# Second head's maxima written into operand rows by a multiply, and a per-partition scalar for the second layer's scale

## The chip, the cores and the metric

The kernel runs on one core of one Trainium2 chip (trn2). The metric is the device time of the whole program in microseconds. Engines are called by their profile names: PE is TensorE (PEld its weight loads), DVE is VectorE, ACT is ScalarE, POOL is GpSimd, SP is SyncE, which here only issues DMAs. L959 is line 959 of the kernel before.

## The reference

Masked attention over 2 batches and 8 heads (768 tokens, 64 columns a head), in which a query sees the keys of its own cluster alone, then two dense layers on the 1536 tokens.

```python
def _attn_ref(q, k, v, centroids):                     # q, k, v: (2, 8, 768, 64)
    q_assign = argmax(einsum(q_n, c_n)); k_assign = argmax(einsum(k_n, c_n))   # 16 clusters
    mask = q_assign[:, :, :, None] == k_assign[:, :, None, :]
    scores = np.where(mask, scale * q @ k.T, -1e9)
    scores = scores - np.max(scores, axis=-1, keepdims=True)
    attn = np.exp(scores)
    attn = attn / (np.sum(attn, axis=-1, keepdims=True) + 1e-09)
    return attn @ v

def _moe_ref(x, w_in, w_out):                          # x: (1536, 512), inner width 2048
    h = x @ w_in
    g = h * (1.0 / (1.0 + np.exp(-1.702 * h)))
    return g @ w_out

def _moe2_ref(x, w_in, w_out, g_ln):                   # inner width 1024
    h = x @ w_in
    e = np.exp(h - np.max(h, axis=-1, keepdims=True))
    solu = h * (e / (np.sum(e, axis=-1, keepdims=True) + 1e-09))
    mu, var = mean and variance of solu along its row
    return (((solu - mu) / np.sqrt(var + 1e-06) * g_ln) @ w_out)
```

## The kernel before

The attention works on 16 heads `u` (pairs `p = u // 2`). Keys and queries of a head lie in two operand tiles, with the tokens along the free dimension: `OP1` holds the high parts of K and Q in partitions 0 to 63, the cluster rows in 64 to 79 and rows for the maxima from partition `KR` = 96 on; `OP2` holds the mixed high and low parts. A pair's operand tiles are used again two pairs later. A head is cut into `NU` = 9 units `m` of 512 columns. For each head the kernel first finds the maximum of each query's masked scores: nine products `peak` (L903, tile `sm`) and nine reductions `peak_max` (L914), then `peak_all` (L922) joins them to a 128x6 tile `nm` and `peak_turn` (L926) turns it on PE to 6x128.

From there the heads differ. Head 0 multiplies the turned tile with the identity, so that row `KR + j` of its Q operand holds the maxima of block `j` and zeros elsewhere (`peak_rows`, L931, on DVE). It does this in two steps, the first four blocks after six of nine units, the rest after all nine. Its scores then contract over rows 0 to `KE` = 102. Every other head copies the turned tile to `mr` (`peak_copy`, L943), and SP moves it by a DMA of 3 KB into one row, `KR` (`peak_row`, L947, recorded at L644 by the helper `move`); its scores contract over 97 rows. The rows of K that face them hold ones, in all six rows of all four operand tiles (L502). The subtraction of the maximum thus happens inside the score products (`score`, L958 and L959, tile `st`). ACT takes the exponential (L967) and casts it to a half precision high part (L972), POOL or DVE subtracts to get the low part (L976), and `value` (L991 to L995) multiplies both with V.

The order of all this is made by a planner at build time. Each operation is a task with a cost per engine, a due time and predecessors (`add`); `Plan.order` takes at each step the earliest possible task, by due time among those that are ready together, keeps account of the PSUM banks (`take`), and emits each engine's queue in that order. The engines then run their queues strictly in order. A changed task can change the order of everything behind it until the attention and the first layer's first three groups of tokens end. The maxima of head `u` are due about one head ahead of its scores (`n0 = (u - 1) * NU - LEAD`).

Behind the planner's part stand loops whose order is written out. `project` (L1308) is the first layer's second product, `solu` (L1372) the second layer's activation, on one tile `t` of 128 tokens (`NT` = 12 tiles). The last loop (L1487) emits per tile: `products(t)`, 48 matmuls on PE; `flip(t - 2)`, the DMA transposes of the finished tile, from SP (for the last tile PE transposes, L1425); `store(t - 3)`, 48 matmuls, the scaling on ACT (L1449) and the DMA out; then `solu(t)`. In `solu`, DVE reduces the maximum (L1376, L1378), multiplies it by the scale `r` of the token group (L1379), ACT takes the exponential with it as bias (L1383), DVE makes 1/sum (L1385, L1388), multiplies by `r` (L1389) and forms the product and its sum (L1392, L1396), ACT sums the squares (L1402), DVE and POOL make the root (L1404 to L1407), DVE normalises (L1408), ACT casts (L1410), and POOL subtracts to get the low part (L1412; DVE for the last tile). Each of these waits for the one before it. `r` comes from `factor` (L1351), which multiplies two [128, 1] columns of a scalar tile once per group (L1356).

Of the kernel before, what the change touches and what calls it, by code (L numbers as in the profile page):

```python
# [15 lines left out]
ALU = mybir.AluOpType  # L16
# [5 lines left out]
def kernel(  # L22
# [21 lines left out]
    nc = tc.nc  # L44
    P = 128
# [12 lines left out]
    KR = 96  # L58
# [22 lines left out]
    TXM = 1  # L81
# [2 lines left out]
    VDA = -20  # L84
    VDB = 1
    LDUE = -8
    URGENT = 0.35
    DEPTH = 1.5
    COLD, WARM = 8.0, 36.0
# [405 lines left out]
    def operands(u):  # L495
        s, i = u // 2 % NS, u % 2
        return OP1[s][i][:, 1, :], OP1[s][i][:, 0, :], OP2[s][i][:, 0, :], OP2[s][i][:, 1, :]
# [418 lines left out]
    def peak_all(u, e=None):  # L916

        n = slice(0, 4 if e == 0 else NJ)
        nms[u] = st_p.tile([P, NJ], F32, tag="nm", name="nm")
        if e == 0:  # L920
            nc.vector.memset(nms[u][:, 4:], 0.0)
        nc.vector.tensor_reduce(out=nms[u][:, n], in_=nma[u][:, n], op=ALU.min, axis=AX.X)  # L922
# [2 lines left out]
        t["tile"] = bank(t)  # L925
        nc.tensor.transpose(t["tile"][0:NJ, 0:P], nms.pop(u), ident)  # L926

    def peak_rows(t, e):

        a, b = (0, 4) if e == 0 else (4, NJ)  # L930
        nc.vector.tensor_tensor(  # L931
            out=operands(0)[0][KR:KE, a * P:b * P].rearrange("p (j n) -> p j n", n=P),
            in0=t["tile"][0:NJ, 0:P].rearrange("p (o n) -> p o n", o=1).to_broadcast([NJ, b - a, P]),
            in1=ident[0:NJ, a:b].rearrange("p (j o) -> p j o", o=1).to_broadcast([NJ, b - a, P]),
            op=ALU.mult,
        )
# [14 lines left out]
    def score(t, u, m):  # L951

        Q1, K1, Q2, K2 = operands(u)
        t["tile"] = bank(t)
        n = KE if u == 0 else KR + 1
        for kt, cs, at in cut(m):
            ks = slice(kt * P, (kt + 1) * P)
            nc.tensor.matmul(t["tile"][:, at], K2[:, ks], Q2[:, cs], start=True, stop=False)  # L958
            nc.tensor.matmul(t["tile"][:, at], K1[0:n, ks], Q1[0:n, cs], start=False, stop=True)  # L959
# [75 lines left out]
    def peaks_of(u):  # L1035
        p, i = divmod(u, 2)
        n0 = (u - 1) * NU - LEAD if u else -40
        ready = [T["PH", p, i]] + [T["PC", p, i, s] for s in range(2)]
        for m in range(NU):
            a = T["SM", u, m] = add(  # L1040
                dict(PE=0.21), n0 + m, lambda t, m=m: peak(t, u, m), after=ready + ([T["PC", 0, 0, 2]] if u == 0 and (m > 5 or m % 3 == 2) else []),
                take="sm",
            )
            T["SX", u, m] = add(
                dict(DVE=0.63), n0 + m + 1, lambda t, m=m, a=a: peak_max(a, u, m),
                after=[a, at("NM", u - 2), T["SX", u, m - 1] if m else None], frees=a,
            )
        for e in range(2 if u == 0 else 0):
            n = 6 if e == 0 else NU
            a = T["NM", u] = add(  # L1050
                dict(DVE=0.13), n0 + n, lambda t, e=e: peak_all(u, e), after=[T["SX", u, m] for m in range(n)] + [at("RW", u)],
            )
            a = T["TR", u] = add(dict(PE=0.06), n0 + n - 4, lambda t: peak_turn(t, u), after=[a], take="tx")
            T["RW", u] = T["RW", u, e] = add(
                dict(DVE=0.35 + 0.25 * (1 - e)), n0 + n - 4, lambda t, a=a, e=e: peak_rows(a, e), after=[a], frees=a
            )
        if u:
            a = T["NM", u] = add(
                dict(DVE=0.07), n0 + NU, lambda t: peak_all(u),
                after=[T["SX", u, m] for m in range(NU)] + [at("TR", u - 2)],  # L1060
            )
            a = T["TR", u] = add(dict(PE=0.06), n0 + NU + -1, lambda t: peak_turn(t, u), after=[a], take="ex")
            a = add(
                dict(ACT=0.25, DVE=0.2), n0 + NU + 1, lambda t, a=a: peak_copy(dict(a, eng=t["eng"]), u),
                after=[a, at("RW", u - 1)], frees=a,
            )
            T["RW", u] = add(dict(SP=(0.65, 0.05)), n0 + NU - 18, lambda t: peak_row(u), after=[a, at("ST", u - 4, NU - 1)])
# [3 lines left out]
    def scores_of(u):  # L1071
        p, i = divmod(u, 2)
        for m in range(NU):
            n = u * NU + m
            d = n if u else n - SOON
            a = T["ST", u, m] = add(
                dict(PE=0.47), d, lambda t, m=m: score(t, u, m),
                after=[T["RW", u, int(m % 3 == 2)] if u == 0 else T["RW", u]] + [T["PB", p, i, e] for e in range(2)], take="st" if u or m >= TXM else "tx",
            )
            o = a  # L1080
            a = T["EX", n] = add(
                dict(ACT=0.5), d, lambda t, m=m, a=a: exponential(a, u, m),
                after=[a] + ([] if stays(n) else held[-NP32:][:1] if len(held) >= NP32 else []), frees=None if stays(n) else a,
            )
            a = add(
                dict(ACT=0.52) if stays(n) else dict(ACT=0.52, DVE=0.36), n + 2, lambda t, m=m: cast(t, u, m),
                after=[a, at("AV", n - NPH)], tail=not stays(n), shared=True,
            )
            T["RE", n] = add(
                dict(DVE=0.62) if stays(n) else dict(POOL=1.11), n + 1, lambda t, m=m: rest(t, u, m), after=[a],  # L1090
                frees=o if stays(n) else None, tail=not stays(n),
            )
            if not stays(n):
                held.append(T["RE", n])
            todo.append((u, m))
            if m in ENDS:
                g = list(todo)
                todo.clear()
                head = [x for x, y in g if y == 0]
                a = add(  # L1100
                    dict(PE=AVC * len(g)), n + ADUE, lambda t, g=g: [value(t, *x) for x in g],
                    after=[T["RE", x * NU + y] for x, y in g] + [T["VL", x // 2] for x, _ in g] + [at("AV", g[0][0] * NU + g[0][1] - 1)],
                    take="av" if head else None, tail=True, kind="av",
                )
                for x, y in g:
                    T["AV", x * NU + y] = a
# [244 lines left out]
    def factor(t):  # L1351

        n = t * P // TB
        if n not in rho2:
            rho2[n] = scalar()
            nc.vector.tensor_tensor(out=rho2[n], in0=rho[n], in1=w2.i, op=ALU.mult)  # L1356
        return rho2[n]

    def products(t):
# [12 lines left out]
    def solu(t, hs):  # L1372
# [3 lines left out]
            nc.vector.tensor_reduce(out=m2[:, i], in_=h, op=ALU.max, axis=AX.X, negate=True)  # L1376
        nm = s_p.tile([P, 1], F32, tag="nm2", name="nm2")
        nc.vector.tensor_reduce(out=nm, in_=m2, op=ALU.min, axis=AX.X)  # L1378
        nc.vector.tensor_tensor(out=nm, in0=nm, in1=r, op=ALU.mult)  # L1379
        e = slots[:, t % NL, :]  # L1380
        sm = s_p.tile([P, 2], F32, tag="sm2", name="sm2")
        for h, s, i in hs:
# [3 lines left out]
            out=ri, in0=sm[:, 0:1], scalar1=sm[:, 1:2], scalar2=1e-9, op0=ALU.add, op1=ALU.add  # L1386
        )
        nc.vector.reciprocal(ri, ri)  # L1388
        nc.vector.tensor_tensor(out=ri, in0=ri, in1=r, op=ALU.mult)  # L1389
        tot = s_p.tile([P, 2], F32, tag="tot", name="tot")  # L1390
        for h, s, i in hs:
            nc.vector.scalar_tensor_tensor(  # L1392
# [142 lines left out]
```

## Time and profile before

| | |
|---|---|
| median of 3 runs | 630.42 us |
| lowest, highest | 629.82, 632.25 us |
| the profiled execution's own time | 631.68 us |
| its span, first to last instruction | 629.9 us |
| busy: PE, DVE, ACT, POOL | 604.0, 456.9, 391.8, 250.0 us |
| mean granted clock of TensorE | 0.992 |

The busy times are sums over stages of different kinds: attention to about 235 us, the first layer to about 510 us (its last stretch mixed with the second layer's first tiles), the second layer to the end. PE's busy time is 96% of the span, but a PE in an idle stretch or at a lower granted clock costs time, and such stretches are few and lie in two places, near the end and between 40 and 52 us. A row of a timeline gives start, duration, engine, line, operation and tiles, and in brackets the idle time before it and what ended that.

### The profile page before, as it was taken

What the parts mean: (1) busy time and instruction counts of PE and PEld (TensorE: products, weight loads), DVE (VectorE), ACT (ScalarE), POOL (GpSimd) and SP (SyncE); (2) the same over time, 40 slices, a digit from 0 to 9 for tenths busy, and PEclk for the clock granted to TensorE, in tenths of its full rate; (3) what the DMA queues carried; (4) which work ended last, traced back from release to release, by engine and by line L of the source; (5) the groups of instructions that cost most, each with busy time, mean ns of one, the idle gap of its engine ahead of it and who ended that gap; (6) DMA issues with size and microseconds to landing.
All of it is one profiled execution on the core that took longest, in us unless ns stands there. A gap on an engine that the chain in (4) does not pass through costs nothing. (4 is left out here: it accounts for less than half of the span.)

```text
span 629.9 us, 12832 instructions
## 1 busy us (share of the span) xinstructions
PE 604.0 (96%) x4879; PEld 395.5 (63%) x4879; DVE 456.9 (73%) x1003; ACT 391.8 (62%) x782; POOL 250.0 (40%) x215
## 2 busy tenths in 40 slices
PE   7989999999999989999999999999999999999977
PEld 6767787888888765556654666666665544444424
DVE  6878989999898858999988033566866356566662
ACT  3589998999999986678777035435335334443432
POOL 8139998758678971224221015200000212222220
PEclk9998999999999999999999999999999999999989
DMA  5897977879797116444520000260500312524241
GB/s 139 203 234 154 211 150 172 191 168 192 163 189 166 44 39 169 143 139 163 170 99 1 1 2 2 67 199 3 167 1 1 34 34 54 98 50 101 51 101 50
DMA packets 78786, 67.93 MB, mean 108 GB/s; under 512 B 61642, under 2 KB 64548, under 8 KB 78724
## 3 DMA queue, kind: packets, MB, share of 16 engines
q1 hardware_dynamic: 78724, 67.11, 44.9%
q8 instruction: 38, 0.62, 0.4%
q14 instruction: 24, 0.20, 0.1%
HBM read 34.64 MB, written 3.15 MB: 60 GB/s over the span
## 5 line engine op out<-in xcount | busy, mean ns | idle before, releaser
L976 POOL TENSOR_TENSOR ph<-p,ph 128x512 f16<-128x512 f32 x115 | 139.4, 1233 | 49.2 <-ACT ph L972 28.4
L1316 PE MATMUL yps<-g,reg 128*128 128x384 f16 x768 | 127.6, 326 | 1.0 <-DVE reg L232 0.9
L1156 PE MATMUL hps<-xT,reg 128*128 128x384 f16 x768 | 126.2, 326 | 1.5 <-DVE g L1167 1.5
L1316 PEld LDWEIGHTS <-reg 128*128 128x128 f16 x768 | 74.7, 98 | 52.4 <-DVE reg L232 4.4
L1156 PEld LDWEIGHTS <-reg 128*128 128x128 f16 x768 | 75.0, 98 | 50.5 <-issue 1.7
L914 DVE TENSOR_REDUCE nma<-sm 128x1 f32<-128x512 f32 x144 | 96.3, 680 | 8.4 <-PE sm L903 7.8
L1177 POOL TENSOR_TENSOR g<-g,g 128x384 f16<-128x384 f32 x40 | 41.7, 1044 | 123.8 <-ACT g L1172 123.8
L967 ACT ACTIVATE p<-st 128x512 f32<-128x512 f32 x114 | 68.6, 609 | 6.4 <-PE st L959 5.2
L958 PE MATMUL st<-OP 128*128 128x256 f32 (+1 forms) x191 | 69.3, 374 | 2.5 <-ACT p L967 1.3
L1406 POOL TENSOR_TENSOR rs<-va,mhalf 128x1 f32<-128x1 f32 x12 | 6.6, 551 | 158.9 <-DVE va L1404 158.9
L972 ACT CAST ph<-p 128x512 f16<-128x512 f32 x109 | 67.4, 630 | 0.4
L1365 PE MATMUL h<-reg,xT 128*128 128x512 f16 x288 | 64.1, 379 | 0.0
L959 PE MATMUL st<-OP 97*128 97x512 f32 (+3 forms) x191 | 63.0, 342 | 0.0
L995 PE MATMUL av<-vh,ph 128*128 128x65 f16 x576 | 61.1, 195 | 1.6 <-POOL ph L976 1.6
L991 PE MATMUL av<-vh,ph 128*128 128x65 f16 x576 | 61.9, 194 | 0.0
L994 PE MATMUL av<-vh,ph 128*128 128x64 f16 x576 | 61.2, 193 | 0.0
L991 PEld LDWEIGHTS <-ph 128*128 128x128 f16 x576 | 52.8, 99 | 11.2 <-issue 9.5
L903 PE MATMUL sm<-OP 80*128 80x512 f32 x192 | 57.6, 361 | 1.6 <-DVE nma L914 0.8
L1441 PEld LDWEIGHTS <-g 128*128 128x128 f16 x312 | 30.7, 99 | 39.0 <-DMA g<-g 6.6
L995 PEld LDWEIGHTS <-ph 128*128 128x128 f16 x576 | 53.6, 97 | 2.0 <-POOL ph L976 2.0
L994 PEld LDWEIGHTS <-ph 128*128 128x128 f16 x576 | 53.7, 97 | 0.2
L208 ACT ACTIVATE junk<-reg 128x512 bf16<-128x512 f32 x48 | 30.4, 633 | 30.8 <-DVE reg L198 18.6
(193 smaller groups left out, 1067.6 us busy)
## 6 DMA issues: line engine op xcount, KB each, us to landing
OP<-hl SPq DMA_DIRECT2D x48, 384.0 KB
raw<-in_moe_w_in_dram SPq DMA_DIRECT2D x24, 512.0 KB
raw<-in_moe_w_out_dram SPq DMA_DIRECT2D x24, 512.0 KB
xT<-in_v_dram SPq DMA_DIRECT2D x8, 384.0 KB
out_dram<-ob SPq DMA_DIRECT2D x11, 256.0 KB
raw<-in_k_dram SPq DMA_DIRECT2D x14, 192.0 KB
raw<-in_q_dram SPq DMA_DIRECT2D x14, 192.0 KB
OP<-oht SPq DMA_DIRECT2D x30, 48.0 KB
```

Of the source, the lines that this page charges most:

```text
L914: nc.vector.tensor_reduce(out=out, in_=src, op=ALU.max, axis=AX.X, negate=True)
L958: nc.tensor.matmul(t["tile"][:, at], K2[:, ks], Q2[:, cs], start=True, stop=False)
L959: nc.tensor.matmul(t["tile"][:, at], K1[0:n, ks], Q1[0:n, cs], start=False, stop=True)
L967: nc.scalar.activation(p32s[u, m], t["tile"], AF.Exp, scale=SCALE)
L972: e(phs[u, m][:, 0], p32s[u, m])
L976: e.tensor_tensor(out=phs[u, m][:, 1], in0=p32s.pop((u, m)), in1=phs[u, m][:, 0], op=ALU.subtract)
L991: nc.tensor.matmul(av[:, i, :], ph[:, 0, qs], vh[:, u, kt, D:], start=(m == 0 and i == 0), stop=False,)
L994: nc.tensor.matmul(av[:, i, 0:D], ph[:, 0, qs], vh[:, u, kt, 0:D], start=False, stop=False)
L995: nc.tensor.matmul(av[:, i, :], ph[:, 1, qs], vh[:, u, kt, D:], start=False, stop=(m == NU - 1 and kt == NJ - 1 and i == NJ - 1),)
L1156: nc.tensor.matmul(self.ps, w1.at(c, m, e), xT[:, x, c, n * TB:(n + 1) * TB], start=(c == 0 and e == x), stop=(c == ND - 1 and e == 1),)
L1316: nc.tensor.matmul(yps, wo.at(f, c, e), lp["g", n][:, x, f, :], start=(f == 0 and e == x), stop=(f == NF - 1 and e == 1),)
L1365: nc.tensor.matmul(h, xT[:, x, c, t * P:(t + 1) * P], w2.half(i * ND + c, e), start=(c == 0 and e == x), stop=(c == ND - 1 and x == 1),)
```

## The change

1. A constant `RWS` = 2 takes the place of "head 0 alone": heads 0 and 1 both have `peak_all` in two steps, two transposes and two `peak_rows`, which write into the head's own operand (`operands(u)`), and both contract their scores over 102 rows. Head 1's `peak_copy` and its DMA `peak_row` are gone. Its score units of the first 512 columns wait for the first of the two steps alone, the others for the second. Head 1's transposes take a PSUM bank of the kind "ex".
2. Three products of [128, 1] columns in the second layer, `tensor_tensor` with two tensors so far, become `tensor_scalar_mul` with the second factor as a per-partition scalar: L1356, L1379 and L1389.

```diff
+    RWS = 2
-    def peak_rows(t, e):
+    def peak_rows(t, u, e):
         a, b = (0, 4) if e == 0 else (4, NJ)
         nc.vector.tensor_tensor(
-            out=operands(0)[0][KR:KE, a * P:b * P].rearrange("p (j n) -> p j n", n=P),
+            out=operands(u)[0][KR:KE, a * P:b * P].rearrange("p (j n) -> p j n", n=P),
...
-        n = KE if u == 0 else KR + 1
+        n = KE if u < RWS else KR + 1
...
-        for e in range(2 if u == 0 else 0):
+        for e in range(2 if u < RWS else 0):
             n = 6 if e == 0 else NU
             a = T["NM", u] = add(
-                dict(DVE=0.13), n0 + n, lambda t, e=e: peak_all(u, e), after=[T["SX", u, m] for m in range(n)] + [at("RW", u)],
-            )
-            a = T["TR", u] = add(dict(PE=0.06), n0 + n - 4, lambda t: peak_turn(t, u), after=[a], take="tx")
+                dict(DVE=0.13), n0 + n, lambda t, e=e: peak_all(u, e), after=[T["SX", u, m] for m in range(n)] + [at("RW", u)] + ([at("TR", u - 2)] if u > 1 else []),
+            )
+            a = T["TR", u] = add(dict(PE=0.06), n0 + n - 4, lambda t: peak_turn(t, u), after=[a], take="ex" if u else "tx")
             T["RW", u] = T["RW", u, e] = add(
-                dict(DVE=0.35 + 0.25 * (1 - e)), n0 + n - 4, lambda t, a=a, e=e: peak_rows(a, e), after=[a], frees=a
-            )
-        if u:
+                dict(DVE=0.35 + 0.25 * (1 - e)), n0 + n - 4, lambda t, a=a, e=e: peak_rows(a, u, e), after=[a], frees=a
+            )
+        if u >= RWS:
...
-                after=[T["RW", u, int(m % 3 == 2)] if u == 0 else T["RW", u]] + [T["PB", p, i, e] for e in range(2)], take="st" if u or m >= TXM else "tx",
+                after=[T["RW", u, int(m % 3 == 2)] if u < RWS else T["RW", u]] + [T["PB", p, i, e] for e in range(2)], take="st" if u or m >= TXM else "tx",
...
-            nc.vector.tensor_tensor(out=rho2[n], in0=rho[n], in1=w2.i, op=ALU.mult)
+            nc.vector.tensor_scalar_mul(rho2[n], rho[n], w2.i)
...
-        nc.vector.tensor_tensor(out=nm, in0=nm, in1=r, op=ALU.mult)
+        nc.vector.tensor_scalar_mul(nm, nm, r)
...
-        nc.vector.tensor_tensor(out=ri, in0=ri, in1=r, op=ALU.mult)
+        nc.vector.tensor_scalar_mul(ri, ri, r)
```

## Rows read from the trace of the kernel before

**Rows 1.** Busy time of each engine in a stretch; granted clock, DMA share, GB/s.
```profile
550.00:600.00 50.00, 50.00 (x233) 22.66 (x232) 31.41 (x72) 21.38 (x37) 13.39 (x10) 1.00 0.33 74
```
**Rows 2.** Timeline of PE, second layer: start, duration, line, tiles, idle before.
```profile
586.66 5.34 PE L1441 MATMUL ops__8050<-reg,g 128*128 128x512 f16 x24
...
597.02 5.34 PE L1441 MATMUL ops__8134<-reg,g 128*128 128x512 f16 x24
...
612.12 1.04 PE L1441 MATMUL ops__8220<-reg,g 128*128 128x512 f16 x2 [4.32 <-DMA g<-g]
613.47 5.44 PE L1441 MATMUL ops__8220<-reg,g 128*128 128x512 f16 x16 [0.31 <-DMA g<-g]
...
619.64 0.62 PE L1425 MATMUL trl<-id,g 128*128 128x128 f16 x8 [0.29 <-DVE g L1412]
```
**Rows 3.** Timeline of DVE, second layer, tiles 10 and 11.
```profile
597.56 1.93 DVE L1379 TENSOR_TENSOR nm<-nm,scl 128x1 f32<-128x1 f32 x1
...
608.12 1.93 DVE L1379 TENSOR_TENSOR nm<-nm,scl 128x1 f32<-128x1 f32 x1
```
**Rows 4.** Line 1379 over the span: least, median and greatest duration in ns.
```profile
L1379 DVE TENSOR_TENSOR nm<-nm,scl x12: 159/1896/1933, 484.0 to 608.1; 128x1 f32<-128x1 f32 x12
```
**Rows 5.** Timeline of POOL, second layer, tile 10.
```profile
607.91 2.12 POOL L1412 TENSOR_TENSOR g<-g,g 128x1024 f16<-128x1024 f32 x1 [2.25 <-issue]
```
**Rows 6.** Timeline of ACT, second layer, the last tiles.
```profile
607.69 0.68 ACT L1449 ACTIVATE ob<-ops__8134,scl 128x512 f32<-128x512 f32 x1
610.08 0.78 ACT L1383 ACTIVATE g<-h,nm,scl 128x512 f32<-128x512 f32 x1 [1.71 <-DVE nm L1379]
```
**Rows 7.** Timeline of SP's queue, second layer, transposes of tile 10.
```profile
608.82 2.68 SPq L1420 DMA_TRANSPOSE g<-g  x2
```
**Rows 8.** Timeline of DVE: narrow operations with a per-partition scalar.
```profile
236.47 0.20 DVE L1137 TENSOR_SCALAR scl<-scl 128x1 f32<-128x1 f32 x1
...
276.17 0.20 DVE L1137 TENSOR_SCALAR scl<-scl 128x1 f32<-128x1 f32 x1
...
47.94 0.44 DVE L1010 TENSOR_SCALAR ri<-ri,scl 128x6 f32<-128x6 f32 x1
```
**Rows 9.** Timeline of POOL beside the operations of the group above.
```profile
235.11 1.87 POOL L976 TENSOR_TENSOR ph<-p,ph 128x512 f16<-128x512 f32 x1
...
275.40 1.14 POOL L1177 TENSOR_TENSOR g<-g,g 128x384 f16<-128x384 f32 x1 [2.23 <-ACT g L1172]
...
47.45 0.91 POOL L768 TENSOR_SCALAR xT<-xT,scl 128x768 f32<-128x768 f32 x1 [6.16 <-DVE scl L794]
```
**Rows 10.** Busy time in two stretches: PE, PEld, DVE, ACT, POOL; clock, DMA.
```profile
30.00:40.00 10.00, 9.17 (x101) 8.01 (x100) 9.35 (x19) 9.67 (x21) 5.61 (x5) 1.00 1.15 304
40.00:50.00 10.00, 8.67 (x87) 6.61 (x86) 6.20 (x21) 6.86 (x14) 3.76 (x4) 0.86 0.80 167
```
**Rows 11.** Timeline of PE, scores of heads 0 and 1 and between them.
```profile
33.25 0.39 PE L959 MATMUL st<-OP 102*128 102x512 f32 x1
...
44.54 0.39 PE L134 MATMUL ex<-vss,ones 128*128 128x8 f32 x2 [0.91 <-ACT vh L756]
...
47.68 0.63 PE L958 MATMUL st<-OP 128*128 128x512 f32 x1
...
51.68 0.39 PE L959 MATMUL st<-OP 97*128 97x512 f32 x1
```
**Rows 12.** Timeline of DVE: the sixth of head 1's nine maxima.
```profile
34.76 0.68 DVE L914 TENSOR_REDUCE nma<-sm 128x2 f32<-128x512 f32 x1
```
**Rows 13.** Timeline of SP's queue: head 1's row of maxima.
```profile
41.56 0.83 SPq L644 DMA_DIRECT2D OP<-mr  x1
```
**Rows 14.** Operations of one line each: least, median, greatest duration in ns.
```profile
L931 DVE TENSOR_TENSOR OP<-tx,ident x2: 417/550/682, 23.8 to 27.0; 6x512 fp32r<-6x512 f32 x1, 6x256 fp32r<-6x256 f32 x1
L922 DVE TENSOR_REDUCE nm<-nma x17: 149/156/166, 22.9 to 213.1; 128x6 f32<-128x12 f32 x16, 128x4 f32<-128x8 f32 x1
L943 DVE CAST mr<-ex x10: 270/278/279, 40.2 to 214.3; 6x128 fp32r<-6x128 f32 x10
```

## The prediction, made before the change was run

> **What bounds the kernel now.** I read the table of engines by stretch first. PE is busy all through the second layer but for its end [rows 1], and for 604.0 us of the 629.9 us span in all (the table of times above), so time can be won only where PE idles, runs at the lower clock, or where something other than PE sets the end. The stretch table shows two such places: 40 to 50 us, and from 608 us on. Next I read PE's timeline at the end. The products of a tile and the store of an earlier one alternate without a gap, one tile every 10.36 us (586.66 to 597.02 us), until the store of tile 10 stands 4.32 us and then 0.31 us for DMA transposes, and the transposes of tile 11 stand 0.29 us for DVE's L1412 [rows 2]. So the last tiles arrive late. The timelines of DVE, ACT and POOL tell why: one tile's activation is a chain in which each step waits for the one before, and its period is 10.56 us (597.56 to 608.12 us) [rows 3], 0.2 us more than PE's. It doesn't catch up, and whatever it is behind after its first tiles, PE pays at the end.
>
> One step of that chain is out of proportion. L1379 multiplies two columns of one element a partition. Its shortest run takes 0.16 us, its median 1.90 us [rows 4]. At tile 11 it starts at 608.12 us, just after POOL's subtraction for the tile before (607.91 us, 2.12 us long), and it ends at 610.05 us, with POOL's end at 610.03 us [rows 3, 5]. ACT stands 1.71 us for it [rows 6]. By the median at least half of the twelve are like this.
>
> **The second edit: the scale as a per-partition scalar.** The question is whether the new form also stands while POOL works. The trace has it: L1137 is a tensor_scalar on 128x1 with a per-partition scalar (it has a second factor, a constant, besides). At 236.47 us it ran in 0.20 us inside POOL's 235.11 to 236.98 us, and at 276.17 us in 0.20 us inside POOL's 275.40 to 276.54 us [rows 8, 9]. It doesn't wait. I take 0.20 us for the new L1379: 1.93 - 0.20 = 1.73 us less on the chain, which then has a period of 10.56 - 1.73 = 8.8 us, under PE's 10.36 us. The chain catches up 1.5 us a tile and from about the middle of the tiles runs at PE's pace. L1356 and L1389 become at most 0.05 us longer each (0.16 to 0.20 us) and hide behind PE for all tiles but the last; I cost them at 0.1 us there at most, within the rounding.
>
> What is late next? On ACT's queue, L1383 of tile 11 stands behind L1449, which scales the store of tile 8. Those matmuls end at 597.02 + 5.34 = 602.4 us [rows 2], while L1449 starts at 607.69 us today [rows 6], since it is queued behind the late chain. With the chain ahead it starts at 602.4 us; 0.68 us later, at 603.1 us, L1383 can start instead of at 610.08 us: 7.0 us earlier. All that follows in the chain of tile 11 keeps its durations and moves with it; PE's last transposes, which wait for L1412, go from 619.64 to 612.6 us. Is PE free by then? The store of tile 9 ends at about 607.5 us. The transposes of tile 10 are issued right after the output that follows L1449; their data let PE go 3.3 us (612.12 us) and 4.65 us (613.47 us) after the issue at 608.82 us [rows 2, 7]. With the issue at 603.6 us that is 606.9 and 608.2 us, so PE stands some 0.4 us instead of 4.6 us. Its 16 matmuls before the transposes took 5.44 us after the long idle time against 24 in 5.34 us for an undisturbed store [rows 2]; at the latter pace they need 3.6 us and end near 611.8 us, ahead of 612.6 us. So the chain still sets the end, by less than 1 us, and the end moves by 7.0 us. If the new form costs nothing at all or the 0.1 us comes on top, this changes by 0.1 us.
>
> A rule speaks against this edit. The Trainium skill ("SBUF — State Buffer", section "Who interferes with whom") says that tensor_scalar too can be blocked by GpSimd, when it enters a mode that uses two ports, and "VectorE: DVE Perf Modes" ("What auto-detection actually checks") gives that mode to a single source in SBUF whose outermost dimensions are even or equal, which one element in and one out could meet. A row bears that out for a wider operation: the 128x6 product L1010 took 0.44 us and ended at 48.38 us beside a POOL operation that ran to 48.36 us [rows 8, 9]. The two rows of L1137 are the nearer ones, 128x1 as here, and they speak against it for one element. By the rule this edit would bring 0.0 us, by the rows 7.0 us; I take the rows.
>
> **The first edit: head 1's rows.** Removed are one copy of 0.28 us and one DMA of 3 KB with 0.83 us of issue on SP [rows 13, 14], ahead of the operand moves queued there. Added on DVE are two products of 0.68 and 0.42 us and one more reduction of 0.15 us [rows 14], in all 1.25 - 0.28 = 0.97 us (a memset of two columns besides), and one more transpose on PE. From 30 to 40 us DVE is busy 9.35 of 10 us [rows 10], so no cover can be claimed for these: I charge 1.0 us in full, and 0.1 us for the transpose (the eight of the row at 619.64 us take 0.62 us [rows 2]). Contracting over 102 rows instead of 97 costs nothing by the rows of both kinds, 0.39 us each for 512 columns [rows 11].
>
> What it frees: head 1's sixth maximum ends at 35.4 us [rows 12], so by the code its scores of the first 512 columns may start about 37.5 us (an estimate: the small steps between, one of each kind in rows 14, are under 2 us together with their hand-overs), where today they wait for all nine, a copy and a DMA issued at 41.56 us [rows 13]. They run from 47.68 us [rows 11]. Between lie 40 to 50 us, with 8.67 us of PE busy and a clock of 0.86, that is, a part of it at the lower level [rows 10]. PE idles 1.33 us there, 0.91 us of it at 44.54 us for ACT [rows 11], and a clock of 0.86 over 10 us costs 1.4 us. Scores ahead of these waits fill them, and since the clock fell here after PE had stood, I expect it to stay up if PE doesn't stand. The most that can be had is thus 2.73 us here, and at most 0.83 us (PE idle from 30 to 40 us) and 0.83 us (SP's issue) more. From below, the planner's order shifts for everything behind; the nearest price of a bad place in it is that of this one, 2.73 us lost. I take 2.73 less the 1.1 us charged: 1.6 us gained, the upper end being nearer because the wait and the rows that end it lie in one stretch. Behind 50 us PE is nearly full, so I let the gain through to the end. Where PE now reaches a score product of the last 256 columns before DVE's second product, it stands with all of its queue behind it, and ACT has nothing to do either; that is in the 2.73 us of the lower bound.
>
> **The sum.** The profiled execution took 631.68 us (span 629.9 us and 1.8 us around it): 631.68 - 7.0 - 1.6 = 623.1 us. It lies 1.26 us above the median of 630.42 us, which gives 621.8 us as the time.
>
> **The rivals.** (a) The gain of the first edit ends at head 2, whose maxima still go through a copy and a DMA: head 1's scores are through earlier and PE waits there instead. For it: only the first row-DMA of fifteen is removed. Against it: DVE and SP are freer from 40 to 50 us than before it (DVE 6.20 of 10 us against 9.35) [rows 10]. Time: 630.4 - 7.0 = 623.4 us, or with the lower bound 2.73 us lost, 626.1 us. Chance 0.27. (b) The edit doesn't do what it says: the multiply stands beside POOL as before, as the 128x6 one of L1010 does, and only the first edit counts: 630.4 - 1.6 = 628.8 us. For it speaks the row of L1010, against it two rows of L1137 [rows 8, 9]. Chance 0.05. It is the case that the two pages named above describe. (c) Slower: the changed planner order makes PE stand, in its strict queue, at scores whose exponential or rows aren't ready, as at 40 to 50 us, each place with 2.73 us of idle time and lower clock. Against the 7.0 us of the second edit it decides from the third such place on (8.2 us, 631.6 us) and is outside 0.5% from the fourth (10.9 us, 634.3 us). Nothing in the rows asks for so many; chance 0.02. (d) The order becomes better also behind 50 us, by more than the bounds above; chance 0.04, under 618.4 us.
>
> **How the numbers follow.** The forecast (both edits gain, 619.0 to 623 us around 621.8 us) has 0.62. The range reaches down to the bounds together, 630.4 - 7.0 - 2.73 - 0.83 - 0.83 = 619.0 us, less 0.6 us for the spread of the runs, and up to the lower end of (a): 618.4 to 626.1 us. Left out are (b), (c), (d) and some of (a), under 0.2. This kernel's measurement can tell about 0.5% from no change, 3.15 us: faster means under 627.27 us. Faster: 0.62 + 0.27 + 0.04 = 0.93; within 0.5%: (b) 0.05; slower: 0.02.
>
> **What would show it.** Right for the second edit: L1379 near 0.2 us in all tiles, L1449 of each store directly behind its last matmul, and no idle time over 1 us on PE after 600 us; wrong: L1379 still ends with POOL. If L1379 is short and PE still idles near the end, the next step that I named is wrong. Right for the first: head 1's scores start before 42 us, no copy to mr for head 1, a clock of 1.00 from 40 to 50 us; wrong: the same idle time some microseconds later. The forecast fails most easily by the planner: PE waits of over 1 us between 50 and 350 us that weren't there.

## The result, and the profile after

| | before | after |
|---|---|---|
| median | 630.77 us (4 runs) | 624.05 us (4 runs) |
| lowest, highest | 629.82, 632.25 us | 623.01, 625.00 us |
| ratio to before, 95% interval | | 0.9864, 0.9830 to 0.9898 |
| the profiled execution's own time, its span | 631.68, 629.9 us | 624.9, 623.1 us |
| mean granted clock | 0.992 | 0.997 |
| busy: PE, DVE | 604.0, 456.9 us | 603.6, 443.7 us |

The change makes the kernel faster by 1.0 to 1.7%. The median lies in the predicted range, 2.2 us above the predicted 621.8 us, and next to the 623.4 us of rival (a), in which the second edit counts and the first brings nothing. Line numbers of the kernel after are those of before plus one.

The second layer's end first. Line 1380 (L1379 of before), then DVE and POOL on one tile, ACT's queue and PE's queue near the end:

```profile
L1380 DVE TENSOR_SCALAR nm<-nm,scl x12: 212/214/215, 484.1 to 601.4; 128x1 f32<-128x1 f32 x12
```
```profile
601.45 0.21 DVE L1380 TENSOR_SCALAR nm<-nm,scl 128x1 f32<-128x1 f32 x1
```
```profile
601.23 2.13 POOL L1413 TENSOR_TENSOR g<-g,g 128x1024 f16<-128x1024 f32 x1 [2.25 <-issue]
```
```profile
602.58 0.69 ACT L1450 ACTIVATE ob<-ops__8138,scl 128x512 f32<-128x512 f32 x1 [1.48 <-PE ops__8138 L1442]
603.17 0.77 ACT L1384 ACTIVATE g<-h,nm,scl 128x512 f32<-128x512 f32 x1
```
```profile
597.15 5.34 PE L1442 MATMUL ops__8138<-reg,g 128*128 128x512 f16 x24
602.33 5.34 PE L1442 MATMUL ops__8184<-reg,g 128*128 128x512 f16 x24
607.66 0.60 PE L1442 MATMUL ops__8224<-reg,g 128*128 128x512 f16 x2
608.89 3.63 PE L1442 MATMUL ops__8224<-reg,g 128*128 128x512 f16 x16 [0.63 <-DMA g<-g]
612.36 1.06 PE L1426 MATMUL trl<-id,g 128*128 128x128 f16 x16
...
617.17 2.78 PE L1442 MATMUL ops__8299<-reg,g 128*128 128x256 f16 x24
```

The multiply lasts 0.21 us in all twelve tiles (least, median and greatest 212, 214 and 215 ns) where it lasted 1.90 us by the median [rows 4], and it does so inside POOL's 601.23 to 603.36 us. The scaling of the store of tile 8 now waits for its own matmuls (the release is PE, 1.48 us of idle time before it) instead of standing behind a late chain [rows 6], and the last exponential starts at 603.17 us instead of 610.08 us. PE stands 0.63 us for the transposes of tile 10 instead of 4.32 and 0.31 us [rows 2]. Its 16 final transposes run without a gap from 612.36 us on; before, the first eight started at 618.74 us and the other eight, which wait for DVE's last subtraction (L1412), at 619.64 us [rows 2]. That subtraction now ends at 612.72 us. The first eight of before, and the subtraction of after:

```profile
618.74 0.61 PE L1425 MATMUL trl<-id,g 128*128 128x128 f16 x8
```
```profile
611.49 1.23 DVE L1413 TENSOR_TENSOR g<-g,g 128x1024 f16<-128x1024 f32 x1 [1.11 <-ACT g L1411]
```

The clock has a part in this. In the kernel before, the stretch behind PE's stand of 4.32 us ran with a granted clock of 0.63:

```profile
612.00:619.00 7.00, 6.57 (x23) 2.38 (x24) 3.71 (x11) 2.88 (x4) 0.55 (x1) 0.63 0.12 22
```

In the kernel after, the clock is 1.00 from 612 us to the end. The 16 matmuls that took 5.44 us [rows 2] take 3.63 us, so that 1.8 us of the gain are these matmuls at the higher clock, beside 4.0 us less of idle time before them.

Now the attention around the first edit: busy time by stretch, in the order PE, PEld, DVE, ACT, POOL, then clock and DMA, to be read against [rows 10].

```profile
30.00:40.00 10.00, 9.77 (x114) 8.03 (x113) 8.96 (x20) 9.68 (x21) 5.61 (x5) 1.00 1.16 304
40.00:50.00 10.00, 8.23 (x83) 6.87 (x80) 6.66 (x19) 7.70 (x15) 3.65 (x4) 0.90 0.98 211
50.00:60.00 10.00, 8.69 (x101) 6.27 (x99) 9.68 (x17) 8.96 (x17) 9.05 (x8) 0.93 0.96 167
60.00:70.00 10.00, 9.45 (x84) 7.17 (x85) 10.00 (x26) 7.08 (x14) 9.75 (x8) 1.00 0.40 79
```

PE has more to do from 30 to 40 us than before (9.77 against 9.17), and less than before from 40 to 50 us (8.23 against 8.67). Behind that stand the next two stretches of before:

```profile
50.00:60.00 10.00, 9.29 (x108) 6.84 (x107) 8.65 (x18) 9.21 (x19) 9.57 (x10) 0.97 0.77 170
60.00:70.00 10.00, 9.85 (x115) 8.19 (x111) 9.02 (x25) 9.73 (x19) 8.99 (x8) 1.00 0.76 157
```

Together they are PE 19.14 us before and 18.14 us after, while DVE goes from 17.67 to 19.68 of 20 us. The idle time of PE has moved to where DVE is nearly full. The stretch with the lower clock has not gone: the clock is 0.90 and then 0.93, where it was 0.86 and then 0.97. PE's timeline after shows what it waited for:

```profile
38.87 0.50 PE L959 MATMUL st<-OP 128*128 128x512 f32 x1
...
45.89 0.39 PE L135 MATMUL ex<-vss,ones 128*128 128x8 f32 x2 [1.77 <-ACT vh L757]
...
53.93 0.50 PE L904 MATMUL sm<-OP 80*128 80x512 f32 x1 [0.50 <-DVE nma L915]
...
56.05 0.50 PE L904 MATMUL sm<-OP 80*128 80x256 f32 x2 [0.56 <-DVE nma L915]
...
61.32 0.27 PE L927 MATMUL ex<-ident,nm 128*6 128x128 f32 x1 [0.17 <-DVE nm L923]
61.92 0.74 PE L904 MATMUL sm<-OP 80*128 80x512 f32 x3 [0.33 <-DVE nma L915]
```

Head 1's scores start at 38.87 us instead of 47.68 us [rows 11]. But PE then waits 1.77 us for the cast of V on ACT, and from 53 us on for DVE's reductions (L915), which find the maxima of the next heads. What it waited for from 50 to 80 us, before and after (us in total, times, longest):

```profile
PE sm L903 <- DVE nma L914: 0.2, 1, 0.2
```
```profile
PE sm L904 <- DVE nma L915: 1.4, 3, 0.6
```

**Where the span went.** The first product of the first layer's second half (`project`, L1316 of before) splits the program into the part of the first edit and the part of the second. The rows give its first and last start, before and after:

```profile
L1316 PE MATMUL yps<-g,reg x768: 322/326/337, 334.1 to 503.5; 128*128 128x384 f16 x192
```
```profile
L1317 PE MATMUL yps<-g,reg x768: 322/326/337, 334.2 to 503.6; 128*128 128x384 f16 x192
```

Up to it the kernels need 334.1 and 334.2 us. From it to the end of the span they need 629.9 - 334.1 = 295.8 us and 623.1 - 334.2 = 288.9 us. In the profiled executions the whole gain, 6.9 us, lies behind 334 us, and none ahead of it.

### The profile page after: what moved, and what is told of

It is laid out like the page before. It is cut to its first block, busy times and chain, and to the rows that moved or that the text cites. A ratio compares the mean times of both kernels' runs of the same rounds, so it can differ in the third digit from the quotient of the medians.

```text
span 623.1 us, 12829 instructions
## 1 busy us (share of the span) xinstructions
PE 603.6 (97%) x4881; PEld 395.3 (63%) x4881; DVE 443.7 (71%) x1008; ACT 391.8 (63%) x781; POOL 248.2 (40%) x213
## 4 chain that ended last, share of the span: by engine, by line
PE 49%; DVE 4%; ACT 2%; issue 1%; DMA 0%; SPq 0%; ACTq 0%; DVEq 0%
PE yps L1317 19%; PE hps L1157 11%; PE h L1366 10%; DVE reg L233 1%; ACT reg L230 1%; DVE g L1168 1%; PE ops__8138 L1442 1%; PE ops__8054 L1442 1%; PE ops__7969 L1442 1%; PE ops__7885 L1442 1%; PE ops__7801 L1442 1%; PE ops__7716 L1442 1%; PE ops__7632 L1442 1%; PE ops__7548 L1442 1%; PE ops__7462 L1442 1%; PE ops__8224 L1442 1%
## 5 line engine op out<-in xcount | busy, mean ns | idle before, releaser
L915 DVE TENSOR_REDUCE nma<-sm 128x1 f32<-128x512 f32 (+1 forms) x144 | 96.7, 681 | 8.4 <-PE sm L904 7.8
L973 ACT CAST ph<-p 128x512 f16<-128x512 f32 x106 | 65.0, 626 | 0.3
```

What stands on the lines that cost most here:

```text
L915: nc.vector.tensor_reduce(out=out, in_=src, op=ALU.max, axis=AX.X, negate=True)
L973: e(phs[u, m][:, 0], p32s[u, m])
```

## The experiments

**One edit at a time.** The first kernel has the second edit alone (the constant is 1, so head 1 keeps its copy and its DMA); the second has the first edit alone; the third is the kernel before with one line of the second edit.

```diff
# the second edit alone, against the kernel after
-    RWS = 2
+    RWS = 1
# the first edit alone, against the kernel after (the lines L1357 and L1390 likewise, not shown)
-        nc.vector.tensor_scalar_mul(nm, nm, r)
+        nc.vector.tensor_tensor(out=nm, in0=nm, in1=r, op=ALU.mult)
# one line, against the kernel before
-        nc.vector.tensor_tensor(out=nm, in0=nm, in1=r, op=ALU.mult)
+        nc.vector.tensor_scalar_mul(nm, nm, r)
```

The second edit alone:

> Only the second edit: three products of [128, 1] columns as a per-partition scalar, head 1's row of maxima goes through the copy and the DMA as before. Theory A (all of the measured gain is the second edit; the first brought about nothing): 6.5 to 7.5 us under the kernel before, ratio 0.988 to 0.990, the same as both edits together within 0.7 us; the short multiply 0.2 us in all twelve tiles, PE idle before the store of tile 10 about 0.6 us instead of 4.6 us. Theory B (the first edit brought its 1.6 us and the second less than forecast): 5 us under the kernel before or less, 1.5 us or more over both edits together.

The first edit alone:

> Only the first edit: head 1's maxima are multiplied into rows, the second layer's products stay products of two tensors. Theory A (the gain of the first edit ends at head 2): within 0.7 us of the kernel before; head 1's scores start near 39 us, but head 2's maxima are turned near 61 us as against 59 us before, and the stand of 4.3 us near 608 us is as before. Theory B (the first edit brings its 1.6 us and something else ate it when both were in): 1.2 to 2 us under the kernel before. In both the multiply of the second layer takes 1.9 us beside POOL.

L1379 alone:

> Of the second edit only the product of the maxima with the scale; the other two products stay products of two tensors. Theory A (only this one meets POOL's subtraction): as the whole second edit within 0.4 us, 6.5 to 7.5 us under the kernel before. Theory B (the other two matter at the end, where the chain of the last tile sets the time): 0.4 to 1 us between the two.

Measured against the same runs of the kernel before (median 631.87 us): the second edit alone 0.9904 (0.9877 to 0.9930), the first alone 1.0002 (0.9986 to 1.0019), L1379 alone 0.9915 (0.9886 to 0.9944). So one line of the second edit brings, within the noise, what the whole of it brings, and the first edit alone lies between 0.9 us faster and 1.2 us slower. Its forecast gain of 1.6 us is outside this. The end of its profile is the one of before, though the attention's order is the one of after; the multiply over the span, then PE near the end:

```profile
L1380 DVE TENSOR_TENSOR nm<-nm,scl x12: 159/1892/1931, 484.2 to 608.6; 128x1 f32<-128x1 f32 x12
```
```profile
612.54 1.03 PE L1442 MATMUL ops__8224<-reg,g 128*128 128x512 f16 x2 [4.30 <-DMA g<-g]
```

The stand of 4.30 us is back with the old form of the multiply.

**Both edits and one, side by side.** In comparisons of their own, the kernel after stood at 0.9864 and the second edit alone at 0.9904. To see whether the first edit brings something when the second is there, both ran again with the same runs of the kernel before (median 632.47 us).

> Both edits, run beside the second edit alone and against the same runs of the kernel before, since the two stand so far in comparisons of their own (0.9864 against 0.9904). Theory A (the first edit brings nothing): both edits and the second alone are within 0.2% of each other, near 0.990 of the kernel before. Theory B (the first edit brings its 1.6 us through the end when the second is there): both edits stand 0.25% (1.6 us) or more below the second alone.

> The second edit alone (head 1 keeps its copy and DMA), beside both edits. Theory A: the same time as both edits within 0.2%. Theory B: 1.6 us or more slower than both edits.

Both edits: 0.9872 (0.9843 to 0.9900), median 625.53 us. The second alone: 0.9916 (0.9887 to 0.9945), median 627.74 us. The medians differ by 2.2 us in favour of both, and the intervals overlap by a little. By the figures set down beforehand this is on the side of theory B, and 0.9864 against 0.9904 was a like difference. Most of it goes with the clock. The nine runs of both edits have mean granted clocks from 0.995 to 1.000, five of them 0.999 or more; the twelve of the second alone from 0.989 to 1.000, three of them 0.999 or more. Runs of like clock lie closer. At 0.995 the one run of both edits took 627.07 us and the six of the second alone 626.40 to 627.93 us; at 1.000 the four of both took 623.01 to 625.00 us and the three of the second alone 624.11 to 625.20 us. So a gain at equal clock is not shown, and whether the first edit makes the lower clock come less often when the second is there, or chance did, stays open. The two profiled executions are alike (spans 625.3 and 625.5 us), and so are their halves; the row of the splitting product, of both edits and of the second alone:

```profile
L1317 PE MATMUL yps<-g,reg x768: 323/326/337, 336.3 to 505.7; 128*128 128x384 f16 x192
```
```profile
L1317 PE MATMUL yps<-g,reg x768: 322/326/337, 336.5 to 505.9; 128*128 128x384 f16 x192
```

336.3 + 289.0 and 336.5 + 289.0 us: the second part is the same as in the kernel after within 0.1 us, and the first is 2.1 and 2.3 us longer than the 334.2 us there. The granted clock offers a cause that differs between executions of one kernel. The second edit alone in its first profiled execution (span 622.5 us) and in this one, on another chip:

```profile
40.00:50.00 10.00, 8.19 (x92) 5.99 (x90) 6.07 (x21) 7.14 (x15) 3.69 (x4) 1.00 0.84 166
...
250.00:260.00 10.00, 7.64 (x48) 4.73 (x49) 9.64 (x24) 7.63 (x17) 2.07 (x2) 1.00 0.52 156
```
```profile
40.00:50.00 10.00, 8.63 (x90) 7.12 (x89) 5.67 (x19) 6.60 (x13) 3.62 (x4) 0.83 0.81 166
...
250.00:260.00 10.00, 7.63 (x39) 4.10 (x37) 9.57 (x23) 7.03 (x16) 0.92 (x1) 0.83 0.56 175
```

The clock is 1.00 in both stretches of the one and 0.83 in both of the other (a part of each at 1.2 GHz), and PE had stood alike ahead of it:

```profile
44.88 0.39 PE L135 MATMUL ex<-vss,ones 128*128 128x8 f32 x2 [0.98 <-ACT vh L757]
```
```profile
45.20 0.39 PE L135 MATMUL ex<-vss,ones 128*128 128x8 f32 x2 [1.04 <-ACT vh L757]
```

The chip is not needed for it: six runs of that kernel on the first chip have mean clocks from 0.995 to 1.000 and times from 624.11 us (1.000) to 627.61 us (0.995). Of the seven profiled kernels of this case that have the attention of the kernel before, three had a low clock near 45 to 55 us and four had not; of the six that have the attention of the first edit or a variant of it, five had such a stretch somewhere between 45 and 75 us and one had none. The first edit therefore doesn't remove it.

**Where the first edit's gain ends.** In the kernel after, head 2's maxima are turned at 61.32 us, and its first score product over 97 rows starts at 65.95 us, against 59.0 and 63.05 us before. Three variants move what could hold head 2 back: its maxima get a due time six units earlier; its maxima are multiplied into rows too, so that it needs neither copy nor DMA; all heads' maxima are due four units earlier.

```diff
# head 2 earlier
-        n0 = (u - 1) * NU - LEAD if u else -40
+        n0 = (u - 1) * NU - LEAD - (6 if u == 2 else 0) if u else -40
# three heads
-    RWS = 2
+    RWS = 3
# lead
-    LEAD = 8
+    LEAD = 12
```

> Both edits, and head 2's maxima are due six units earlier in the planner; nothing else differs. Without the first edit this shift leaves the order as it is. Theory P (the first edit's gain ended at head 2's maxima, which the planner's order put too late on DVE and PE): head 2's turned maxima near 58.5 us instead of 61.3 us, the last score product near 230 us instead of 232 us, and 1.5 to 2 us under both edits without it. Theory Q (an earlier end of attention is taken up at the join with the first layer, where DVE is busy with the weights): the last score product is as early, but the first layer's second product starts near 334 us as in all so far, and the time stays within 0.7 us of both edits.

> Both edits, with three heads instead of two whose maxima are multiplied into rows: head 2's copy and DMA are gone too, and its scores of the first 512 columns wait for six maxima only. Theory P1 (the copy and the DMA of head 2 hold the gain of the first edit): head 2's scores start 3 us earlier or more, near 62 us, and the time is 1.5 to 2.5 us under both edits. Theory P2 (what holds it is the work on DVE and PE for head 2's maxima, not the DMA), or Q (the join takes it up): within 0.7 us of both edits.

> Both edits, with the maxima of every head due four units earlier than so far, an order that the planner itself ends about 5 us later; it serves to make the attention longer. Theory Q (the join takes up differences in the end of the attention): the last score product comes 3 to 6 us later than with both edits, the first layer's second product at most half of that later. Theory P (what the attention loses is lost at the end): both come later by the same amount, and the time is longer by it.

Measured, the first two against the same runs of the kernel before (median 632.30 us): head 2 earlier 0.9905 (0.9870 to 0.9941), three heads 0.9918 (0.9889 to 0.9947), lead 630.53 us in one run. Neither ratio is below the 0.9864 and 0.9872 of the kernel after, and the one run of the lead is slower than all nine runs of that kernel. The starts in their profiled executions (us; the second product of a head's first score unit, the first product of the last score unit, the first layer's first product, and the splitting product):

| | head 1 | head 2 | head 3 | last score | first layer | split |
|---|---|---|---|---|---|---|
| before | 48.1 | 63.1 | 76.7 | 230.0 | 233.5 | 334.1 |
| first edit alone | 40.0 | 65.3 | 78.4 | 231.9 | 232.9 | 334.3 |
| after | 39.2 | 66.0 | 78.3 | 231.8 | 232.9 | 334.2 |
| head 2 earlier | 40.3 | 61.8 | 78.9 | 230.9 | 234.4 | 334.9 |
| three heads | 40.2 | 62.2 | 79.8 | 233.6 | 236.6 | 338.3 |
| lead | 38.5 | 65.0 | 79.8 | 237.4 | 239.6 | 339.9 |

These are single executions. In the seven with the attention of the kernel before, head 3 starts between 75.2 and 78.1 us and the split lies between 332.3 and 336.5 us; in the six with the first edit, head 3 starts between 78.3 and 80.3 us and the split lies between 334.2 and 339.9 us. By head 3, 8 to 10 us of earlier scores of head 1 have turned into none.

Two things more can be read here. First, head 2 can be had 4.2 us earlier, and head 3 then starts at 78.9 us, no earlier than the 78.3 us of the kernel after: the gain goes one head further and ends there. The stretches around its end (head 2 earlier):

```profile
50.00:60.00 10.00, 8.82 (x108) 7.01 (x108) 10.00 (x24) 9.34 (x17) 9.83 (x9) 1.00 0.79 174
60.00:70.00 10.00, 8.69 (x101) 7.29 (x101) 9.74 (x24) 9.26 (x18) 9.83 (x9) 1.00 0.76 158
70.00:80.00 10.00, 9.32 (x84) 7.50 (x83) 9.22 (x17) 5.86 (x12) 7.97 (x7) 0.83 1.00 220
```

DVE is at 10.00 and 9.74 of 10 us, POOL at 9.83 in both, PE at 8.82 and 8.69. With head 2's maxima ahead, PE idles beside a full DVE and POOL all the same, and the low clock has come to 70 to 80 us. That head 2's maxima alone carry the loss is refuted by this run. Second, the attention of the kernel after ends 1.8 us later than before, and the first layer starts 0.6 us earlier, at the same split: in these two executions the difference is taken up where the two stages meet. It isn't always: with the lead of 12 the attention ends 5.6 us later than in the kernel after and the split is 5.7 us later; with three heads 1.8 us become 4.1 us, with a clock of 0.66 from 255 to 260 us besides. So the join hides a small shift in some orders and not in others, and which part of it does so stays open.

**What the multiply waits for.** Whether only one element per partition escapes POOL, and by which property, is what the following kernels ask. In two of them the scale is applied to the two column minima, before they are joined, once as they are (128x2) and once with a third column that holds 1e30 (128x3). In the last, which stands on the second edit alone, the joining and the scaling are one operation on 128x1 with two per-partition scalars. The scale is positive, so it may be applied ahead of the minimum.

```diff
# two columns, against the kernel before
+        nc.vector.tensor_scalar_mul(m2, m2, r)
         nc.vector.tensor_reduce(out=nm, in_=m2, op=ALU.min, axis=AX.X)
-        nc.vector.tensor_tensor(out=nm, in0=nm, in1=r, op=ALU.mult)
# three columns, besides
-        m2 = s_p.tile([P, 2], F32, tag="m2", name="m2")
+        m2 = s_p.tile([P, 3], F32, tag="m2", name="m2")
+        nc.vector.memset(m2[:, 2:3], 1e30)
# one operation, against the second edit alone
-        nc.vector.tensor_reduce(out=nm, in_=m2, op=ALU.min, axis=AX.X)
-        nc.vector.tensor_scalar_mul(nm, nm, r)
+        nc.vector.tensor_scalar(out=nm, in0=m2[:, 0:1], scalar1=m2[:, 1:2], scalar2=r, op0=ALU.min, op1=ALU.mult)
```

> The kernel before, with the scale multiplied into the two half maxima (128x2, per-partition scalar) and the smaller of the two taken after it; the sum of operations is the same, only the width of the tensor_scalar differs from the change. Theory A (one column doesn't wait for POOL, an even width does, as the 128x6 product in attention): the multiply ends with POOL's subtraction, about 2.0 us in nine tiles, and the time is that of the kernel before within 1 us. Theory B (the form alone decides: a tensor_scalar with a per-partition scalar never waits here): 0.2 us in all tiles and 6.5 to 7.5 us under the kernel before.

> As the run with two columns, with a third column that is set to 1e30 and so never the smaller one: the scale is multiplied into 128x3, an odd width. Theory A (every width over one waits for POOL): about 1.9 to 2.1 us in nine tiles, time as the kernel before or up to 2 us over it (one small operation more on the chain). Theory B (only even widths wait): 0.2 us in all tiles, 5.5 to 7.5 us under the kernel before.

> The second edit alone, and L1378 and L1379 as one tensor_scalar on 128x1 whose two scalars (the other column's minimum, the scale) both come per partition. If one element per partition doesn't wait for POOL, however many per-partition scalars it takes, the operation lasts 0.2 us in all 12 tiles, the chain is 0.15 us shorter, which lies behind PE for all tiles but the last: the same time as the second edit alone, less 0.2 us at most. If a second per-partition scalar makes it wait, it lasts up to 2.1 us and ends with POOL's subtraction, and the time is that of the kernel before.

The line of the multiply over the span and DVE beside POOL at tile 11, for two columns:

```profile
L1378 DVE TENSOR_SCALAR m<-m,scl x12: 228/2089/2131, 483.9 to 609.6; 128x2 f32<-128x2 f32 x12
```
```profile
609.61 2.12 DVE L1378 TENSOR_SCALAR m<-m,scl 128x2 f32<-128x2 f32 x1
```
```profile
609.59 2.12 POOL L1412 TENSOR_TENSOR g<-g,g 128x1024 f16<-128x1024 f32 x1 [2.25 <-issue]
```

for three columns:

```profile
L1379 DVE TENSOR_SCALAR m<-m,scl x12: 228/2078/2119, 482.0 to 607.7; 128x3 f32<-128x3 f32 x12
```
```profile
607.70 2.11 DVE L1379 TENSOR_SCALAR m<-m,scl 128x3 f32<-128x3 f32 x1
```
```profile
607.66 2.12 POOL L1413 TENSOR_TENSOR g<-g,g 128x1024 f16<-128x1024 f32 x1 [2.25 <-issue]
```

and for the one operation with two scalars:

```profile
L1379 DVE TENSOR_SCALAR nm<-m,scl x12: 272/273/276, 486.1 to 603.4; 128x1 f32<-128x1 f32 x12
```
```profile
603.42 0.27 DVE L1379 TENSOR_SCALAR nm<-m,scl 128x1 f32<-128x1 f32 x1
```
```profile
603.40 2.12 POOL L1412 TENSOR_TENSOR g<-g,g 128x1024 f16<-128x1024 f32 x1 [2.25 <-issue]
```

With two or three elements the operation is the same `tensor_scalar` with the same scalar. In nine of the twelve tiles it lasts 2.0 to 2.1 us and ends with POOL's subtraction (at tile 11 at 611.73 and 611.71 us with two elements, at 609.81 and 609.78 us with three); in the first three, with no POOL operation beside it, it lasts 0.23 us. With one element it lasts 0.27 us beside the same POOL operation, with two per-partition scalars. The times go with it: two columns 1.0034 (1.0013 to 1.0054) of the kernel before, three columns 631.61 us in one run (median of before 632.30 us), one operation 0.9906 (0.9875 to 0.9938), no different from the second edit alone in the same comparison (0.9916). So a `tensor_scalar` in float32 waits here with more than one element per partition, whether the number is even or odd; a `tensor_tensor` waits with one element too. The thirteen traces bear this out more widely: of 938 float32 `tensor_scalar` operations on 128x1, some with constants alone as factors, 122 overlap a POOL operation by more than 0.05 us, and none lasts longer than 0.28 us, while those on 128x6 reach 1.63 us.

## Why the prediction was right, and where it was wrong

**The second edit: mechanism and size right.** The step that decided, from two rows of L1137, was that a 128x1 product with a per-partition scalar doesn't stand beside POOL [rows 8, 9]; the multiply lasts 0.21 us, forecast 0.20 us. The steps behind it came out one by one: L1449 forecast to start at 602.4 us, measured 602.58; the last exponential 603.1 and 603.17 us; PE's stand before the store of tile 10 0.4 and 0.63 us; that store's 16 matmuls 3.6 and 3.63 us. One sentence behind them does not hold as it stands: that the chain still sets the end, because the final transposes wait for DVE until 612.6 us. They start at 612.36 us straight behind the 16 matmuls, and PE stands for nothing there; DVE's subtraction ends at 612.72 us, just ahead of the ninth transpose at 612.80 us. The end of PE's own work and the end of the chain lie within 0.4 us of each other, and the forecast is as good by either. The last store moved from 624.02 us, by the row of before

```profile
624.02 2.78 PE L1441 MATMUL ops__8295<-reg,g 128*128 128x256 f16 x24
```

to 617.17 us, 6.85 us earlier, where 7.0 us were forecast. The whole of it came through, because the next thing that is late, PE itself, had been costed beside the chain. Rival (b) falls with the multiply's row. Of the rule of the Trainium skill that the prediction weighed against those rows ("SBUF — State Buffer", "Who interferes with whom": tensor_scalar too can be blocked by GpSimd, in a mode that uses two ports), the runs with 128x2 and 128x3 show 2.1 us and so bear it out; the 128x1 form, 0.21 us, lies outside it. The condition that the prediction took from the Trainium skill's "VectorE: DVE Perf Modes" ("What auto-detection actually checks") is there one on the outermost non-unit dimensions; the prediction left out "non-unit", and one element per partition has no such dimension, so that page does not say that this form enters the mode. L1010's 128x6 was the right row for the rule and the wrong one for this edit.

**The first edit: the step that failed** is "Behind 50 us PE is nearly full, so I let the gain through to the end". What that step took for evidence was PE's row alone. The forecast of the front was good: scores expected from 37.5 us start at 38.87 us, and head 1's copy and DMA are gone. But PE's idle time didn't go away. It went to 40 to 70 us, from 53 us on in front of DVE's reductions, and DVE is at 19.68 of 20 us from 50 to 70 us. In that stretch the DVE row of before, 17.67 of 20 us, left 2.3 us, and 2.0 of them were used. Pieces of work moved into the stretch and out of it. Among them, in the kernel after the planner gives DVE one piece of V's low part that POOL did before, and just ahead of the stretch a narrow product of two tensors stands longer,

```profile
48.67 0.95 DVE L795 TENSOR_TENSOR scl<-scl 128x1 f32<-128x1 f32 x1
...
50.22 1.58 DVE L772 SCALAR_TENSOR_TENSOR vh<-xT,scl,vh 128x768 f16<-128x768 f32 x1
```

the first of them 0.14 us long in the kernel before (L794). Together they are 2.4 us more, the size of the 2.3 us by which head 2's maxima are late, but no run isolates them: with head 2 earlier no V piece lies on DVE, and PE idles beside a full DVE still. What is shown is that head 1's earlier scores bring nothing that can be seen at the split, in any of the orders that were tried. Rival (a) named this end and gave head 2's copy and DMA as its cause. They do cost head 2 its start (three heads: 62.2 instead of 66.0 us), but without them nothing is gained either, since head 3 then starts at 79.8 us. What the orders share is that PE waits for DVE: of its waits from 50 to 80 us, 1.6 us are put down to DVE in the kernel after, 2.1 us with the first edit alone, 2.6 us with head 2 earlier, 2.3 us with three heads and 1.8 us with the lead, against 0.2 us in the kernel before. A full DVE they do not share: with three heads it is busy 8.00 and 8.94 of 10 us from 50 to 70 us, at clocks of 0.75 and 0.91. That DVE's load is the cause is therefore argued and not shown; no run took work off DVE.

The other term that failed is the clock's. Of the 2.73 us that the stretch from 40 to 50 us was said to hold, 1.4 us were the low clock. The kernel with the second edit alone has the same attention and had a clock of 1.00 there in one execution and 0.83 in another. One profiled execution can't say whether such a stretch belongs to the kernel. Of the signs that the prediction named for the first edit, the scores before 42 us came, and head 1's copy is gone, but the clock of 1.00 from 40 to 50 us did not come: it was 0.90. The sign for being wrong, the same idle time later, came in its place: PE stands 1.77 us for ACT until 45.89 us, where it had stood 0.91 us until 44.54 us, and for DVE behind that.

**The sum.** Forecast -7.0 - 1.6 us, measured -6.9 us behind the split and +0.1 us ahead of it in the profiled executions: 631.68 - 6.8 = 624.9 us. The median of 624.05 us is the sum with the first edit at zero, 623.4 us, within 0.7 us. It lies in the range although one of its two terms failed, since the range was made to reach down to rival (a). Whether the first edit adds up to 2.2 us of gain when the second is there, by way of the clock, isn't settled by the side-by-side runs; alone it doesn't.

**The chances.** The case with both gains had 0.62, rival (a) 0.27. The rows of DVE from 50 to 70 us, 17.67 of 20 us busy, which the prediction did not read, left little room there and so spoke for (a).

## What to carry to other kernels

A narrow operation whose median is ten times its shortest run is probably waiting, and when its end coincides with another engine's, look for a form that doesn't wait beside that engine; here a row of the same shape elsewhere in the trace told more about it than a rule for wider ones. When PE is let forward in one stretch, read in the next stretches not PE's row alone but that of every engine that feeds it: a gain can end at the first one that has no room. An earlier start of one stage is worth what the last stage's end moves, so look at a point behind both (here the split) before counting it.

## What the runs showed of the hardware

- A `tensor_scalar` of float32 with a per-partition scalar took 0.21 us on 128x1 beside a POOL subtraction of 2.13 us, and 2.12 and 2.11 us on 128x2 and 128x3 beside one of 2.12 us, ending within 0.03 us of POOL; the shortest runs of the wider ones took 0.23 us. With two per-partition scalars it took 0.27 us, and did not wait either. A `tensor_tensor` on 128x1 does wait (1.90 us by the median, 0.16 us at the shortest).
- The same kernel ran with a granted clock of 1.00 from 40 to 50 us in one execution and of 0.83 in another after 0.98 and 1.04 us of idle time of PE. By the split's row the second needed 336.5 us to it and the first 333.6 us; the second had another such stretch, 250 to 260 us. That the two cost the 2.9 us together is an estimate: two executions without any low clock ahead of the split differ by 1.3 us there (332.3 us with three columns, 333.6 us here).
- After PE had stood 4.32 us, until 612.12 us, 16 matmuls took 5.44 us in a stretch with a granted clock of 0.63; after 0.63 us of idle time they took 3.63 us at 1.00.
